# Local attention's forward scores: two heads at a time into two buffers, or four heads into one buffer of four banks

## The chip, the cores and the metric

The kernel runs on one core of one Trainium2 chip. The metric is the device time of one execution in microseconds (us); the kernel before has a median of 2354.34 us over three runs (2354.0 to 2360.47). Smaller is better. A profile is one execution taken by the hardware profiler; its times are given from the start of its span.

The engines are called by the profile's names: PE (matrix multiplication; PEld is its loading of weights, which overlaps), DVE (vector), ACT (scalar; it computes the exponentials), POOL (GpSimd) and SP, which here only issues DMAs. PSUM is the memory that PE writes its results to; it has 8 banks of 512 fp32 columns in each of 128 partitions.

## The reference

Four layers, A, B, A, B, each with a layer norm and a residual, on x of 2048 tokens by 640 features, 32 heads of 20, and then the gradients of all of it for a given gradient of the output. A is linear attention, B is causal softmax attention over a window of 256 tokens. The forward pass of B is the part that the change touches:

```python
scores = jnp.einsum("bhqd,bhkd->bhqk", q, k) * (Dh ** -0.5)
idx = jnp.arange(S)
mask = (idx[:, None] - idx[None, :] >= 0) & (idx[:, None] - idx[None, :] < W)   # W = 256
scores = jnp.where(mask[None, None], scores, -1e9)
p = _softmax(scores, axis=-1)
o = jnp.einsum("bhqk,bhkd->bhqd", p, v)
return (lambda x, *d: x.transpose(*d))(o, 0, 2, 1, 3).reshape(B, S, D) @ wo

x = A_x
x = x + _A_ref(_layernorm(x, axis=-1), A_wqkv, A_wo)
x = x + _B_ref(_layernorm(x, axis=-1), B_wqkv, B_wo)
x = x + _A_ref(_layernorm(x, axis=-1), A_wqkv, A_wo)
x = x + _B_ref(_layernorm(x, axis=-1), B_wqkv, B_wo)

_out, _vjp = jax.vjp(_f, A_x, A_wqkv, A_wo, B_wqkv, B_wo)
_grads = _vjp(grad_out)
```

## The kernel before, in words

The tokens are cut into 16 tiles of 128 rows (`TT`), and the forward pass walks over the tiles in three stretches. The first normalises each tile for layer 0 and makes its q, k and v (`a_first`, `a_qkv`). Then `ab_pass(0, False)` finishes layer 0 and does layer 1 tile by tile, and meanwhile starts layer 2 with `a_first(items, l + 2, ...)`. Last, `ab_pass(2, True)` finishes layer 2 and does layer 3; it starts no following layer, but the flips of the weights (`wflips`) that the backward pass needs belong to it. The two calls of `ab_pass` are called pass 0 and pass 2 here, by the layer they begin with.

For one tile, a pass has these pieces, each with its line: the linear attention's result (`a_num`, matmuls of L528 and of L389, `mm_ps<-mbd,pqT`), its output projection (`out_proj` with `Wo_A`, residual add L555), the layer norm (`ln`, L417 to L427), the six 320-column chunks of q, k and v of the local attention (`b_qkv`, matmuls L389 with `Wqkv_B`, evacuated by ACT L580 and DVE L578), the attention itself (`attn`), and its output projection with `Wo_B`. In pass 0 six chunks with `Wqkv_A` of the next layer stand beside them (ACT L453 and L444, DVE L454, L457 and L447). Operands are turned by DMA transposes on SP's queue (`flip`, L361).

`attn` works on a tile of 128 queries and at most three tiles of keys (`nkt` is 1 for the first tile, 2 for the second, then 3). A head has 20 features, padded to 32 rows, so that four heads, a group `g`, lie in the 128 partitions of one slice, head `hh` in the rows from 32 `hh`. There are 8 groups, `G`. A group was handled as two pairs, `p_` = 0 and 1, in these steps:

- `scores(g, p_)`: six matmuls (L605), each 128 keys by 128 queries over 32 rows, at `tile_position=(32 hh, 0)`, the two heads in two PSUM banks of an `s_ps` buffer, of which there are two; ACT's exponential of the 768 columns (L612) into an `e_sb` buffer, of which there are five; the triangular mask on the last key tile by a select on POOL (L615); the mask on the first key tile by a select on POOL for the second pair (L619), and by a multiplication with `maskT_first` on DVE for the first pair (L623).
- `values(g, p_)`: six matmuls (L646; two heads by three key tiles) of the exponentials with v, to which a column of ones is added, into one PSUM bank `pv_ps` for 16 heads. After 16 heads DVE takes the reciprocal of the sums (L653) and multiplies (L654) into `oB`, so each of these stands twice in a tile.

PSUM's eight banks are: three `mm_ps`, two `s_ps` of two banks each, one `pv_ps`. In the first stretch (layer 0) some chunks and transposes also use the `s_ps` buffers (`turn` with "s", `a_qkv`'s chunks 0 and 2).

The order is planned when the program is built. Each piece is recorded with `op(engine, duration, function, reads, writes)`; pieces get a time in units of tiles (`spread`, `items`), are sorted by it, and `Sched.order` then lays the operations out on the engines by estimated durations, an operation of PE not more than 12 places ahead of the order of priority (`AHEAD`). A `Ring` is a set of buffers used in turn; the first operation of a use waits for all operations of the use `n` places earlier. What comes out is a fixed order for each engine, and each engine carries its instructions out in that order. The planned times do not exist at run time; only the order and the semaphores do. In it, `attn`'s scores of tile `tt` are spread over the time from `tt` to `tt + 1`, and its values are the same but later by a lag of 2.1 (pass 0) or 3.1 (pass 2) of 16 steps:

```python
for part in (0, 1):
    lag = 0.001 + part * (3.1 if last else 2.1) / (2 * G)
    spread(items, tt + lag, tt + lag + 1.0, [att(i, part) for i in range(2 * G)])
```

The backward passes (from L800 on; `B_attn_bwd` has its own scores at L1324 and exponentials at L1344) are not touched.

## Time and profile before

| | |
|---|---|
| runs | 2354.34, 2354.0, 2360.47 us |
| the profiled execution | 2355.23 us, its span 2353.3 us, mean granted PE clock 0.961 |
| forward pass | 0 to about 785 us |
| pass 0, pass 2 | 148 to 484 us, 484 to 780 us |
| score matmuls L605 | 2880, 170.1 us busy |
| exponentials L612 | 512, 381.3 us busy; 813 ns with 768 columns (448 of them), 598 with 512, 385 with 256 |
| POOL's selects L615, L619 | 512 of 441 ns, 224 of 407 ns |
| DVE's mask multiplication L623 | 224 of 294 ns |
| values matmuls L646 | 2880, 148.4 us busy |

How to read it: busy times overlap across engines, and a matmul's record runs from its start to the end of its pipeline, so matmuls that follow one another overlap in the records as well. A row of the stretch windows gives the stretch, its length, each engine's busy time with its number of instructions, the granted PE clock (1.00 is full speed), the mean busy share of the DMA engines and what they moved in GB/s. A row of the timeline gives start and length in us, the engine, the line, and how many instructions of that kind follow one another; in square brackets is the idle time before it and what ended it.

### The profile page before, as it was taken

What the parts mean: (1) busy time and instruction counts of PE and PEld (TensorE: products, weight loads), DVE (VectorE), ACT (ScalarE), POOL (GpSimd) and SP (SyncE); (2) the same over time, 40 slices, a digit from 0 to 9 for tenths busy, and PEclk for the clock granted to TensorE, in tenths of its full rate; (3) what the DMA queues carried; (4) which work ended last, traced back from release to release, by engine and by line L of the source; (5) the groups of instructions that cost most, each with busy time, mean ns of one, the idle gap of its engine ahead of it and who ended that gap; (6) DMA issues with size and microseconds to landing.
All of it is one profiled execution on the core that took longest, in us unless ns stands there. A gap on an engine that the chain in (4) does not pass through costs nothing. (4 is left out here: it accounts for less than half of the span.)

```text
span 2353.3 us, 69243 instructions
## 1 busy us (share of the span) xinstructions
PE 2116.3 (90%) x28146; PEld 1438.8 (61%) x28146; DVE 1462.1 (62%) x3121; ACT 1239.7 (53%) x2093; POOL 854.1 (36%) x1852
## 2 busy tenths in 40 slices
PE   6989999879999888989889989997989888997889
PEld 4656666555555557777756557744777775664664
DVE  6756666555555579998833329803898994443552
ACT  4537777627788258888722213313888882210330
POOL 1015444405556345555512203302555551220110
PEclk9989999989999799999999989997999999998999
DMA  7759999526686867767687779637776677988973
GB/s 259 222 126 208 203 214 212 135 90 150 142 163 153 230 146 123 134 126 135 137 186 171 174 160 212 149 90 155 134 126 130 127 144 153 190 177 189 195 149 101
DMA packets 937072, 377.93 MB, mean 161 GB/s; under 512 B 817072, under 2 KB 921136, under 8 KB 936496
## 3 DMA queue, kind: packets, MB, share of 16 engines
q1 hardware_dynamic: 856672, 299.45, 63.1%
q10 hardware_dynamic: 80080, 74.06, 9.9%
q8 instruction: 220, 3.60, 0.7%
q14 instruction: 100, 0.82, 0.1%
HBM read 115.34 MB, written 114.95 MB: 98 GB/s over the span
## 5 line engine op out<-in xcount | busy, mean ns | idle before, releaser
L1344 ACT ACTIVATE e_sb<-pair 128x768 bf16<-128x768 f32 x480 | 389.0, 812 | 123.9 <-PE pair L1324 116.4
L1359 DVE TENSOR_TENSOR ds_sb<-pair,e_sb 128x768 bf16<-128x768 f32 x480 | 436.3, 948 | 18.2 <-PE pair L1324 13.7
L612 ACT ACTIVATE e_sb<-s_ps 128x768 bf16<-128x768 f32 (+2 forms) x512 | 381.3, 772 | 98.1 <-PE s_ps L605 43.0
L615 POOL TENSOR_SCALAR_AFFINE_SELECT e_sb<-e_sb 128x256 bf16<-128x256 bf16 x512 | 225.7, 441 | 466.8 <-ACT e_sb L612 461.6
L841 PE MATMUL mm_ps<-wq,dqT 128*128 128x320 bf16 x1920 | 286.9, 305 | 21.6 <-DMA dqT<-dqkv 20.2
L841 PEld LDWEIGHTS <-om 128*128 128x128 bf16 x1920 | 190.6, 100 | 170.1 <-DMA om<-o 12.9
L1351 POOL TENSOR_SCALAR_AFFINE_SELECT e_sb<-e_sb 128x256 bf16<-128x256 bf16 x448 | 182.1, 406 | 270.0 <-ACT e_sb L1344 261.3
L841 PE MATMUL mm_ps<-dqkv,om 128*128 128x480 bf16 x1280 | 271.4, 370 | 0.0
L1007 POOL TENSOR_TENSOR gw<-w,gcar 128x640 f32<-128x640 f32 x64 | 89.4, 1398 | 480.3 <-ACT w L1004 474.8
L841 PEld LDWEIGHTS <-dqT 128*128 128x128 bf16 x1920 | 187.4, 100 | 99.9 <-DMA dqT<-dqkv 24.2
L1348 POOL TENSOR_SCALAR_AFFINE_SELECT e_sb<-e_sb 128x256 bf16<-128x256 bf16 x512 | 206.4, 406 | 78.7 <-ACT e_sb L1344 77.3
L989 ACT ACTIVATE dh<-mm_ps 128x320 f32<-128x320 f32 x128 | 55.9, 437 | 334.3 <-PE mm_ps L841 290.6
L1388 PE MATMUL dqvk_ps<-Ksl,dsT 128*128 128x32 bf16 x2880 | 223.2, 177 | 3.0 <-DVE dqkv L1397 3.0
L1392 PE MATMUL dqvk_ps<-Qsl,ds_sb 128*128 128x32 bf16 x2880 | 220.2, 176 | 0.0
L1392 PE MATMUL dqvk_ps<-dOsl,e_sb 128*128 128x32 bf16 x2880 | 220.1, 176 | 0.0
L1372 PE MATMUL dsT_ps<-ident,ds_sb 128*128 128x128 bf16 x2244 | 192.2, 223 | 28.9 <-ACT dsT L1376 25.0
L1324 PE MATMUL pair<-KTg,QTg 32*128 32x384 bf16 (+2 forms) x1024 | 163.7, 324 | 41.9 <-DVE ds_sb L1359 33.0
L1376 ACT COPY dsT<-dsT_ps 128x768 bf16<-128x768 bf16 x240 | 190.9, 795 | 11.8 <-PE dsT_ps L1372 5.8
L1372 PEld LDWEIGHTS <-ds_sb 128*128 128x128 bf16 x2244 | 139.8, 99 | 92.0 <-issue 88.5
L389 PE MATMUL mm_ps<-Wqkv_B,hnTB 128*128 128x320 bf16 x960 | 179.2, 307 | 2.2 <-DMA hnTB<-hnB 1.9
L605 PE MATMUL s_ps<-QT,KT 32*128 32x128 bf16 x2880 | 170.1, 220 | 7.6 <-ACT e_sb L612 6.8
L1324 PE MATMUL pair<-VTg,dOTg 32*128 32x384 bf16 (+2 forms) x1024 | 163.8, 326 | 13.4 <-DMA dOTg<-dOpt 6.8
(155 smaller groups left out, 3734.7 us busy)
## 6 DMA issues: line engine op xcount, KB each, us to landing
qkvp<-qk_slab SPq DMA_DIRECT2D x32, 512.0 KB, 3.4
o<-o SPq DMA_DIRECT2D x64, 160.0 KB, 3.2
om<-o SPq DMA_DIRECT2D x20, 512.0 KB, 4.8
hn<-hn SPq DMA_DIRECT2D x64, 160.0 KB, 2.8
om<-hn SPq DMA_DIRECT2D x20, 512.0 KB, 5.1
qkvp<-v_slab SPq DMA_DIRECT2D x32, 256.0 KB, 2.7
dOpt<-slab ACTq DMA_DIRECT2D x32, 256.0 KB, 3.3
Ksl<-qkvp SPq DMA_DIRECT2D x16, 512.0 KB, 5.0
```

What stands on the lines that cost most here:

```text
L612: op("ACT", av(2 * nkt * P), lambda: nc.scalar.activation(e.t[:, :, 0:nkt, :], s.t[:, :, 0:nkt * P].rearrange("p h (i q) -> p h i q", q=P) ...
L615: op("POOL", 410, lambda: nc.gpsimd.affine_select(out=e.t[:, :, nkt - 1, :], in_=e.t[:, :, nkt - 1, :], compare_op=ALU.is_ge, fill=0.0, ba ...
L841: nc.tensor.matmul(ps.t[:, w0:w0 + width], lhsT=lhsT(), rhs=rhs(), start=start, stop=stop)
L1324: nc.tensor.matmul(ps[:, i, c0:c0 + len(ks) * P], lhsT=ld[g][lhs][r, q * P:(q + 1) * P], rhs=ld[g][rhs][r, ks[0] * P:(ks[-1] + 1) * P], st ...
L1344: nc.scalar.activation(e, PR[h][:, :, 0:3 * P].rearrange("p i (j q) -> p i j q", q=P), ACT.Exp, scale=self.c_att)
L1348: nc.gpsimd.affine_select(out=e[:, :, j, :], in_=e[:, :, j, :], compare_op=ALU.is_ge, fill=0.0, base=0, pattern=[[0, 2], [-1, P]], channel ...
L1351: nc.gpsimd.affine_select(out=e[:, :, j, :], in_=e[:, :, j, :], compare_op=ALU.is_ge, fill=0.0, base=-1, pattern=[[0, 2], [1, P]], channel ...
L1359: nc.vector.tensor_mul(DS[n][:, hs], PR.pop(h)[:, :, 0:3 * P].rearrange("p i (j q) -> p i j q", q=P), E[n][:, hs])
L1372: nc.tensor.transpose(ps[:, i, j, :], DS[n][:, 2 * p + i, j, :], self.ident)
L1376: (nc.vector.tensor_copy if h % 2 else nc.scalar.copy)(TSB[h], TPS.pop(h))
L1388: nc.tensor.matmul(a[:, 0, hh, :], lhsT=TSB[2 * n + hh // 2][:, hh % 2, j, :], rhs=ld[g]["K"][:, k, cs], start=(i == 0), stop=(i == len(dq ...
L1392: nc.tensor.matmul(a[:, 1 + x, hh, :], lhsT=src[n][:, hh, j, :], rhs=ld[g][rhs][:, q, cs], start=(i == 0), stop=(i == len(dkv) - 1))
```

## The change

Pairs are gone. `scores(g)` issues twelve matmuls, for each of the three key tiles the four heads in turn, into one PSUM tile `s_ps` of four banks; one exponential reads 1536 columns of it; then come the two triangular selects, each for two heads, the multiplication on DVE for the first two heads and the select of the first key tile for the other two. `values(g, p_)` stays, a pair at a time, and its reads name the half of the exponentials that it needs. The PSUM tile is a single buffer: its ring has one place. `e_sb` becomes three buffers of four heads. In the first stretch the same four banks serve as two halves (`halves`), and `follows` makes the first use of the whole tile wait for the last uses of the halves. The lag of the values becomes 3.1 steps in both passes, with 8 score pieces and 16 values pieces to a tile. An unused mask, `maskT_last`, goes, and `ones_bf` shrinks to the columns that are read.

```diff
@@ -43,8 +43,9 @@
 class Ring:
...
-    def __init__(self, n, make=None, tiles=None, name=""):
+    def __init__(self, n, make=None, tiles=None, name="", follows=None):
         self.n, self.make, self.tiles, self.items, self.name = n, make, tiles, [], name
+        self.follows = follows
...
                 if not b.ops and b.idx >= b.pool.n:
                     o.deps.update(b.pool.items[b.idx - b.pool.n].ops)
+                elif not b.ops and b.pool.follows is not None:
+                    for c in b.pool.follows.items[-b.pool.follows.n:]:
+                        o.deps.update(c.ops)
                 b.ops.append(o)
...
             PS = dict(space=bass.MemoryType.PSUM)
-            mmp, sp_ = pool("mm_ps", 3, **PS), pool("s_ps", 2, **PS)
+            mmp = pool("mm_ps", 3, **PS)
+            s_ps = pool("s_ps", **PS).tile([P, 4, 512], F32, name="s_ps")
+            halves = Ring(2, tiles=[s_ps[:, 2 * i:2 * i + 2, :].rearrange("p a b -> p (a b)") for i in range(2)])
             R = dict(
-                s=Ring(2, make=lambda: sp_.tile([P, 2, 512], F32, name="s_ps"), name="s_ps"), pv=ring("pv_ps", 1, [P, 16, 32], F32, **PS),
+                half=halves, s=Ring(1, tiles=[s_ps], follows=halves), pv=ring("pv_ps", 1, [P, 16, 32], F32, **PS),
                 mm=Ring(3, make=lambda: mmp.tile([P, 512], F32, name="mm_ps"), name="mm_ps"),
-                e=ring("e_sb", 5, [P, 2, 3, P]), QT=ring("QT", 2, [P, G, P]), KT=ring("KT", 5, [P, G, P]),
+                e=ring("e_sb", 3, [P, 4, 3, P]), QT=ring("QT", 2, [P, G, P]), KT=ring("KT", 5, [P, G, P]),
...
                     def f():
                         c0 = ci * CW
-                        ps = R["s" if l == 0 and ci in (0, 2) else "mm"].buf()
-                        if l == 0 and ci in (0, 2):
-                            ps.make = lambda: sp_.tile([P, 1024], F32, name="s_ps")
+                        ps = R["half" if l == 0 and ci in (0, 2) else "mm"].buf()
...
                 o = R["oB"].buf()
                 pvs, lv, es = {}, R["li"].buf(), {}
 
-                def products(g, p_, s):
-                    def mm_s():
-                        for j in range(nkt):
-                            for i, hh in enumerate((2 * p_, 2 * p_ + 1)):
-                                r = slice(HPAD * hh, HPAD * (hh + 1))
-                                nc.tensor.matmul(s.t[:, i, j * P:(j + 1) * P], lhsT=kTs[j].t[r, g, :],
-                                                 rhs=qT.t[r, g, :], start=True, stop=True,
-                                                 tile_position=(HPAD * hh, 0))
-                    op("PE", 200 + 50 * nkt, mm_s, [qT] + kTs, [s])
-
-                def weights(g, p_, s):
-                    e = es[g, p_] = R["e"].buf()
-                    op("ACT", av(2 * nkt * P), lambda: nc.scalar.activation(
-                        e.t[:, :, 0:nkt, :], s.t[:, :, 0:nkt * P].rearrange("p h (i q) -> p h i q", q=P),
-                        ACT.Exp, scale=self.c_att), [s], [(e, j) for j in range(nkt)])
-                    op("POOL", 410, lambda: nc.gpsimd.affine_select(
-                        out=e.t[:, :, nkt - 1, :], in_=e.t[:, :, nkt - 1, :], compare_op=ALU.is_ge, fill=0.0, base=0,
-                        pattern=[[0, 2], [1, P]], channel_multiplier=-1), [], [(e, nkt - 1)])
-                    if nkt == 3 and p_ == 1:
-                        op("POOL", 410, lambda: nc.gpsimd.affine_select(
-                            out=e.t[:, :, 0, :], in_=e.t[:, :, 0, :], compare_op=ALU.is_ge, fill=0.0, base=-1,
-                            pattern=[[0, 2], [-1, P]], channel_multiplier=1), [], [(e, 0)])
-                    elif nkt == 3:
-                        op("DVE", v2(2 * P), lambda: nc.vector.tensor_mul(
-                            e.t[:, :, 0, :], e.t[:, :, 0, :],
-                            self.maskT_first.unsqueeze(1).to_broadcast([P, 2, P])), ["masks"], [(e, 0)])
-
-                def scores(g, p_):
+                def scores(g):
                     def f():
                         s = R["s"].buf()
-                        products(g, p_, s)
-                        weights(g, p_, s)
+
+                        def mm_s():
+                            for j in range(nkt):
+                                for hh in range(4):
+                                    r = slice(HPAD * hh, HPAD * (hh + 1))
+                                    nc.tensor.matmul(s.t[:, hh, j * P:(j + 1) * P], lhsT=kTs[j].t[r, g, :],
+                                                     rhs=qT.t[r, g, :], start=True, stop=True,
+                                                     tile_position=(HPAD * hh, 0))
+                        op("PE", 210 + 55 * nkt, mm_s, [qT] + kTs, [s])
+                        e = es[g] = R["e"].buf()
+                        op("ACT", av(4 * nkt * P), lambda: nc.scalar.activation(
+                            e.t[:, :, 0:nkt, :], s.t[:, :, 0:nkt * P].rearrange("p h (i q) -> p h i q", q=P),
+                            ACT.Exp, scale=self.c_att), [s], [(e, p_, j) for p_ in (0, 1) for j in range(nkt)])
+                        for p_ in (0, 1):
+                            op("POOL", 440, lambda p_=p_: nc.gpsimd.affine_select(
+                                out=e.t[:, 2 * p_:2 * p_ + 2, nkt - 1, :], in_=e.t[:, 2 * p_:2 * p_ + 2, nkt - 1, :],
+                                compare_op=ALU.is_ge, fill=0.0, base=0, pattern=[[0, 2], [1, P]],
+                                channel_multiplier=-1), [], [(e, p_, nkt - 1)])
+                        if nkt == 3:
+                            op("DVE", v2(2 * P), lambda: nc.vector.tensor_mul(
+                                e.t[:, 0:2, 0, :], e.t[:, 0:2, 0, :],
+                                self.maskT_first.unsqueeze(1).to_broadcast([P, 2, P])), ["masks"], [(e, 0, 0)])
+                            op("POOL", 410, lambda: nc.gpsimd.affine_select(
+                                out=e.t[:, 2:4, 0, :], in_=e.t[:, 2:4, 0, :], compare_op=ALU.is_ge, fill=0.0, base=-1,
+                                pattern=[[0, 2], [-1, P]], channel_multiplier=1), [], [(e, 1, 0)])
                     return f
 
                 def values(g, p_):
                     def f():
-                        e = es.pop((g, p_))
+                        e = es[g]
                         q = 4 * g // 16
                         if q not in pvs:
                             pvs[q] = R["pv"].buf()
                         pv = pvs[q]
 
                         def mm_pv():
-                            for i, hh in enumerate((2 * p_, 2 * p_ + 1)):
+                            for hh in (2 * p_, 2 * p_ + 1):
                                 h = 4 * g + hh
                                 for j in range(nkt):
-                                    nc.tensor.matmul(pv.t[:, h % 16, :], lhsT=e.t[:, i, j, :],
+                                    nc.tensor.matmul(pv.t[:, h % 16, :], lhsT=e.t[:, hh, j, :],
                                                      rhs=vts[j].t[:, h, :], start=(j == 0), stop=(j == nkt - 1))
                         op("PE", pe([DH + 1] * 2 * nkt), mm_pv,
-                           [(e, j) for j in range(nkt)] + [(v, c) for v in vts for c in (4, 5)], [pv])
+                           [(e, p_, j) for j in range(nkt)] + [(v, c) for v in vts for c in (4, 5)], [pv])
                         if g % 4 == 3 and p_ == 1:
                             h0 = 16 * q
                             li = lambda: lv.t[:, h0:h0 + 16]
...
                             dma("ACT", lambda: self.tm_view(self.sv[l]["linv"])[:, b, :], lambda: lv.t, 16 * KB,
                                 [(lv, i) for i in range(H // 16)], [])
                     return f
-                gp = [(g, p_) for g in range(G) for p_ in (0, 1)]
-                return [scores(*a) for a in gp], [values(*a) for a in gp]
+                return [scores(g) for g in range(G)], [values(g, p_) for g in range(G) for p_ in (0, 1)]
 
             def spread(items, t0, t1, fs):
...
                         items.append((tt - 21 / 12 + i / 6, len(items), out(i)))
                         items.append((tt + 23 / 12 + i / 6, len(items), outb(i)))
                     spread(items, tt - 1.0, tt, [qkv(i) for i in range(6)])
-                    for part in (0, 1):
-                        lag = 0.001 + part * (3.1 if last else 2.1) / (2 * G)
-                        spread(items, tt + lag, tt + lag + 1.0, [att(i, part) for i in range(2 * G)])
+                    for part, lag in ((0, 0.001), (1, 3.1 / (2 * G))):
+                        spread(items, tt + lag, tt + lag + 1.0, [att(i, part) for i in range((1 + part) * G)])
                 if last:
                     spread(items, 2.0, 13.0, [wflips(t, i) for t in "BA" for i in range(4 * DT)])
                 else:
```

## The prediction

> **What bounds the kernel now.** I read the page first for where TensorE is full, then the stretch windows, then the timeline inside one tile. The change touches only the forward pass, which ends near 785 us (the last score product of `s_ps` starts at 777.5 us), the first third of these slices:
>
> ```profile
> span 2353.3 us, 69243 instructions
> ...
> PE   6989999879999888989889989997989888997889
> ...
> ACT  4537777627788258888722213313888882210330
> ...
> DMA  7759999526686867767687779637776677988973
> ```
>
> Local attention runs twice: in pass 0 (148 to 484 us, shared with the next layer's projections) and in pass 2 (484 to 780 us). Stretches in steady state, PE, PEld, DVE, ACT and POOL in this order, then clock and DMA:
>
> ```profile
> 300.00:420.00 120.00, 118.63 (x1665) 73.72 (x1663) 81.99 (x234) 94.92 (x166) 59.37 (x142) 1.00 0.97 211
> 660.00:740.00 80.00, 79.91 (x1259) 47.52 (x1257) 46.31 (x135) 66.83 (x105) 48.91 (x120) 1.00 0.75 159
> ```
>
> PE is busy 98.9% and 99.9% at full clock, ACT 79% and 84%. In pass 0 the DMA share is 0.97 too. So TensorE's instruction stream sets the pace. To get the time of a 128-row tile I count the reciprocals of L653, two per tile, with both ends inside each window:
>
> ```profile
> 197.40:404.60 207.20, 5.14 (x21) 1.00 0.97 209
> 404.60:460.40 55.80, 1.64 (x7) 0.97 0.63 151
> 551.80:750.60 198.80, 5.92 (x25) 1.00 0.71 151
> 671.10:735.30 64.20, 2.01 (x9) 1.00 0.74 158
> 750.60:780.00 29.40, 1.02 (x5) 0.76 0.64 198
> ```
>
> 21 reciprocals are ten tiles: 20.7 us each in pass 0, and three more in its tail at 18.6. In pass 2 twelve tiles take 16.6 each, the last four of the steady ones 16.05, and the two at the end 14.7. Inside a tile:
>
> ```profile
> 303.61 0.84 PE L389 MATMUL mm_ps<-Wqkv_B,hnTB 128*128 128x320 bf16 x5
> 304.38 0.34 PE L605 MATMUL s_ps<-QT,KT 32*128 32x128 bf16 x6
> 304.65 0.31 PE L646 MATMUL pv_ps<-v_slab,e_sb 128*128 128x32 bf16 x6
> 304.82 0.84 PE L389 MATMUL mm_ps<-Wo_A,oTA 128*128 128x320 bf16 x5
> 305.59 0.34 PE L605 MATMUL s_ps<-QT,KT 32*128 32x128 bf16 x6
> 305.86 0.32 PE L646 MATMUL pv_ps<-v_slab,e_sb 128*128 128x32 bf16 x6
> ...
> 306.03 0.81 ACT L612 ACTIVATE e_sb<-s_ps 128x768 bf16<-128x768 f32 x1 [0.16 <-PE s_ps L605]
> ```
>
> Rows overlap because a matmul's record includes its latency, so I price by starts. Five 320-column matmuls: one lasts 0.30, so starts are (0.84-0.30)/4 = 0.135 apart. From the start of five to the start of the values matmuls is 1.04 us, twice; less 5 x 0.135 leaves **0.365 us for one score batch**. Only 0.125 of it is streaming (0.34 less the 0.214 that one score matmul lasts; three pairs, about 0.06 a pair). The other 0.24 is spent entering and leaving the 32-row form; the trace shows the same hole as weight loads that stand 0.26 us for no semaphore ("issue", 109.5 us over 393 batches of L605).
>
> **The change, part by part.**
>
> *Score batches.* 16 batches of six matmuls per tile become 8 batches of twelve. Removed: eight entries and exits. The trace has no four row groups at once. Lower bound of the cost: four stream as two do (the members of a pair stand within a few ns of each other), a batch stays 0.365, and a group saves 0.365, a tile 8 x 0.365 = 2.9 us. Upper bound: twelve matmuls stream as six pairs, a batch is 0.365 + 3 x 0.063 = 0.555, and a tile saves 8 x (0.73-0.555) = 1.4 us. I take the lower cost: the pair already shows that matmuls of different row groups do not wait for one another. The Trainium skill, "TensorE: Matmul & The Clock Gate", section Part 3: Packing small matmuls, says that matmuls in distinct 32-row groups run concurrently, about 4 ns apart, and gives 3.07x for four; by it the saving is 2.9 us, by pairs 1.4.
>
> *The exponential.* L612 takes 813 ns for 768 columns and 598 for 512, so 0.84 ns a column; 1536 columns take 813 + 768 x 0.84 = 1.455 us. Two of 768 take 1.51 back to back (570.78 us), so ACT gains next to nothing (0.06 us a group). ACT is not the bound, so I count it at nothing.
>
> *One buffer instead of two.* This is the added wait: scores of group g+1 can start only when the exponential of g has ended. Queued behind the waiting matmul on PE are the values of g, the projections, and with them DVE's and ACT's evacuations. The loop, from rows: exponential 1.455; to the first score matmul about 0.06 (an exponential of 570.78 + 0.81 = 571.59, then this row), batch 0.34, to the next exponential 0.10 (305.59 + 0.34 = 305.93, then 306.03).
>
> ```profile
> 570.78 1.51 ACT L612 ACTIVATE e_sb<-s_ps 128x768 bf16<-128x768 f32 x2 [1.00 <-PE s_ps L605]
> ...
> 571.65 0.34 PE L605 MATMUL s_ps<-QT,KT 32*128 32x128 bf16 x6 [0.20 <-ACT e_sb L612]
> ```
>
> That is 1.95 us a group, 15.6 a tile (2.14 and 17.1 if as pairs). ACT's other work fits in the 0.5 us between exponentials: evacuations of 0.43 us overlap their neighbours by 0.1 at each end.
>
> *Pass 0.* PE alone: 20.7-2.9 = 17.8 us a tile, above the loop's 15.6, and the PE work between two batches in the built order is even (1.64 to 1.94 us a group), so the loop is covered. If the cover failed, each group would pay the excess over 17.8/8 = 2.2 us. What comes near next is DMA. 209 GB/s x 20.7 us = 4.33 MB a tile; the built order carries about half a weight flip less per tile (0.16 MB), so 4.17 MB in 17.8 us is 234 GB/s, against 211 in the longest full stretch and 222 in the fullest 20 us. At 211 a tile takes 19.8 us, at 222 18.8. Bounds 17.8 to 19.8; I take 18.5, because the present stretch has no PE wait for a DMA, so some slack is there. Saving 2.2 x 10 = **22 us**. The tail's three tiles have less to interleave: 18.6 becomes about 17.3, **4 us**.
>
> *Pass 2.* PE alone: 16.05-2.9 = 13.1, so the loop takes over at 15.6. In the built order three of eight groups carry 1.66 us of other matmuls plus 0.365: 2.03, each 0.08 over the loop; a tile is 15.8 at best. Bounds: 15.8 (0.8 under today's 16.6) to 17.1 (as pairs, 0.5 over). I take 16.3: **12 x 0.3 = 4 us** saved. The two last tiles have no projections left to fill with: 14.7 becomes the loop's 15.8, **2 us lost**.
>
> *Moved without cost.* Masks on POOL: the same 24 a tile, 10 us of 18, now in threes of 1.27 us behind each exponential; the values of the second pair wait for the third one and stand after at least one chunk of projections (0.68), which covers most of it. The mask multiply stays one a group on DVE (82 of 120 us busy). Three buffers of four heads hold more than five of two. The later slot of pass 0's values and the layer-0 use of the same banks as two halves add no instruction; SP's and ACT's DMAs are the same in number. The dropped mask saves one 128x128 memset and one POOL select, once.
>
> Sum: -22 -4 -4 +2 = **-28**. The profiled execution took 2355.2 us (span 2353.3 and 1.9 around it), 0.9 over the runs' median of 2354.3: 2327.
>
> **The rivals.**
>
> *Full gain* (12%): DMA gives way and both passes reach their floors. Pass 0 -29, tail -6, pass 2 12 x -0.8 = -10, end +2: 2311. For it: no DMA wait on PE now; against: 0.97.
>
> *DMA takes the place of PE in pass 0* (13%): tile 19.8, so -9, tail -2, pass 2 -2: 2341. For it the share of 0.97 in exactly that stretch, against it that in pass 2 the share is 0.71.
>
> *Four do not run at once* (11%), so the change doesn't do what it says: pass 0 at 19.4, -13, tail -2, pass 2 at the pairs' loop 17.1, +6, end +5: 2350. For it: no row with four groups.
>
> *The single buffer makes it slower* (14%). PE executes in order: if the values of g, waiting for POOL's selects, and a chunk of 0.68 stand ahead of the next scores, the scores come late by d, and nothing else can feed ACT. The third select ends 0.44 + 0.41 + 0.41 = 1.27 us after the exponential (L615, L619); plus values 0.17 and a chunk it is 2.1, so d of 0.2 is near at hand in some groups. A tile is then t = 15.6 + 8d wherever that is the longest. Pass 2 loses from d = 0.12. Over 10 + 3 + 12 + 2 tiles the sum 27t stands against 207.2 + 55.8 + 198.8 + 29.4 = 491, so the whole loses from t = 18.2, d = 0.33. At d = 0.4, t = 18.8: +16, 2370. Against it: the built order spreads this work evenly in pass 0. The Trainium skill, "Perfetto Trace Analysis", section Optimizing Tensor Performance, speaks for it: groups should rotate through different banks so that one's evacuation overlaps the next one's matmuls. Today's trace agrees (PE waits only 6.8 us in 13 places for L612); the change gives just that up.
>
> **How the numbers follow.** Forecast 2327 at 50%, its own range 2315 to 2340. About 0.3% (7 us) can be told from no change. Faster: the forecast, the full gain and most of the DMA case, 0.70. Same: the pairs case and what is left of DMA's, 0.16. Slower: 0.14. Eight in ten: 2306, just under the full gain, to 2360, over the pairs case and short of most of the slower one.
>
> **What would show it.** A score batch of twelve lasts 0.34 to 0.36 us from first start to last end (right), 0.5 or more (pairs). L612 is 256 instructions, 1.455 us at full size. A tile of pass 0 takes 17.8 to 19, with PE still over 95% busy; if PE falls to 90% and waits for flips (`hnTB`, `QT`, `KT`), DMA took over. In pass 2 PE is some 85% busy and its idle time stands before L612's scores, released by ACT; with a tile over 17 us the slower rival is true. What lies behind 790 us should only move, not change. The forecast is wrong at the root if batches cost less than 0.24 us to enter and leave once alone, or if PE's clock, which fell to half at the end of pass 2 (0.76 in the last window above), falls in the steady part with the thinner PE work.

## The result, and the profile after

The changed kernel takes 2366.6 us (median of 7 runs, 2361.5 to 2370.7), the kernel before on the same chip 2354.6 (7 runs): ratio 1.0052, 95% interval 1.0032 to 1.0071. It is slower by half a per cent, where 2327 us was forecast. The profiled execution took 2366.6 us, its span is 2364.9, the mean granted clock 0.957.

From its page, the total and the same three rows of slices:

```profile
span 2364.9 us, 68753 instructions
...
PE   5778888878888789898889979997989888997899
...
ACT  3527777716777328888822213312888882210330
...
DMA  7659999726666766777687779736666677878963
```

TensorE lost its nines in the first third: it is no longer full there, and yet nothing is faster. The stretch windows (PE, PEld, DVE, ACT, POOL, clock, DMA share, GB/s), and two windows of the reciprocals L653:

```profile
300.00:420.00 120.00, 106.49 (x1677) 70.12 (x1675) 82.98 (x238) 88.23 (x120) 59.03 (x144) 0.99 0.95 205
660.00:740.00 80.00, 67.91 (x1180) 46.14 (x1178) 47.67 (x128) 61.96 (x62) 46.91 (x114) 0.96 0.70 141
...
209.60:417.00 207.40, 4.75 (x21) 0.98 0.97 203
574.80:767.00 192.20, 5.83 (x23) 0.95 0.68 144
```

In pass 0 PE falls from 98.9% to 88.7% busy, and 21 reciprocals still take 207 us, ten tiles of 20.7: the work that was saved became waiting. In pass 2, 23 reciprocals are eleven tiles of 17.4 us, where the kernel before took 16.5. That the batches do cost less can be read from the timeline of PE:

```profile
303.72 0.84 PE L394 MATMUL mm_ps<-Wqkv_B,hnTB 128*128 128x320 bf16 x5
304.49 0.35 PE L612 MATMUL s_ps<-QT,KT 32*128 32x128 bf16 x12
304.77 0.43 PE L532 MATMUL mm_ps<-mbd,pqT 128*128 128x320 bf16 x3
```

From 303.72 to 304.77 are 1.05 us; less five chunks' starts of 0.135 a batch of twelve costs 0.375 us. A batch of six cost 0.365.

Cut at the ends of every second reciprocal, the spans divide so (us):

| | to the end of tile 0 | pass 0, 15 tiles | to tile 0 of pass 2 | pass 2, 15 tiles | rest |
|---|---|---|---|---|---|
| before | 166.6 | 293.8 | 77.3 | 242.5 | 1573.0 |
| after | 178.3 | 293.6 | 69.6 | 259.6 | 1563.7 |
| difference | +11.7 | -0.2 | -7.7 | +17.1 | -9.3 |

So there are three questions: why the first stretch grew by 11.7 us although no score is computed there, why pass 0 gained nothing inside, and why pass 2 lost 17.

**First stretch.** PE's rows stand in the same order as before, but it waits at new places. Timeline of PE after:

```profile
30.20 0.57 PE L394 MATMUL s_ps<-Wqkv_A,hnTA 128*128 128x320 bf16 x3 [0.58 <-DVE pp L461]
31.55 0.43 PE L394 MATMUL s_ps<-Wqkv_A,hnTA 128*128 128x320 bf16 x2 [0.78 <-ACT hnTA L416]
```

The second row is the rest of the same five-matmul sum as the first. In the middle of an accumulation it waits for ACT's copy of `hnTA`, which reads the other half of the four banks. The first theory (shared tile): the framework takes the two halves, views of one tile, for one buffer.

**Pass 0.** ACT's timeline with the DMA issues of its queue (ACTq), and one row of SP's queue:

```profile
302.74 1.45 ACT L617 ACTIVATE e_sb<-s_ps 128x1536 bf16<-128x1536 f32 x1
303.75 0.33 ACTq L362 DMA_DIRECT2D r<-rt  x1
306.01 0.34 ACTq L362 DMA_DIRECT2D v<-vv  x1
306.40 0.42 ACT L584 CAST v_slab<-mm_ps 128x320 bf16<-128x320 f32 x1 [2.21 <-PE mm_ps L394]
306.57 0.34 ACTq L362 DMA_DIRECT2D o<-oA  x1
306.72 1.46 ACT L617 ACTIVATE e_sb<-s_ps 128x1536 bf16<-128x1536 f32 x1
...
301.23 1.15 SPq L362 DMA_DIRECT2D WqTA<-wT  x1
```

The scores of 304.49 are done at 304.84, and the exponential starts at 306.72. The bracket blames PE, but what stands in front is the store of `v`, issued at 306.01. The trace has for each DMA the semaphore that tells of its landing. That of `v` is the one that the store `WqTA<-wT` uses too, which landed at 305.92, and `v` is issued 0.1 us after. In the traces all DMAs of the two queues use eight such semaphores in turn, so a store on ACT waits for the landing of the DMA eight places earlier, on whichever queue. Before, `v` followed another store of ACT on its semaphore; after, the new order puts a weight flip or its store there, and `ek` behind the flip `hnTA`. From 195 to 415 us 17 stores of ACT are issued within 0.35 us after such a landing, and ACT had stood idle 22.5 us before them; before there were 6, with 4.0 us. Over 10.6 tiles that is 2.1 us a tile, just what 18.5 lacks to 20.7.

**Pass 2.** ACT again:

```profile
608.26 1.45 ACT L617 ACTIVATE e_sb<-s_ps 128x1536 bf16<-128x1536 f32 x1 [0.60 <-POOL e_sb L621]
609.72 0.33 ACTq L362 DMA_DIRECT2D linv<-li  x1
610.09 0.42 ACT L584 CAST qk_slab<-mm_ps 128x320 bf16<-128x320 f32 x1 [0.38 <-DVE li L653]
610.25 1.23 ACTq L362 DMA_DIRECT2D o<-oB  x1
611.60 1.45 ACT L617 ACTIVATE e_sb<-s_ps 128x1536 bf16<-128x1536 f32 x1 [1.08 <-DVE x L559]
```

The next scores are done at 610.11. But the store of `o` takes 1.23 us to issue, and the next exponential, queued behind it, starts 1.89 us after the last one's end. The second theory (held queue): with one buffer nothing but the next exponential lets PE go on, and ACT's queue carries stores that hold it. The rival for pass 0 is the prediction's own: transfers, at a share of 0.95 to 0.97, bind.

### The profile page after: what moved, and what is told of

Same layout as the page of the kernel before. It is cut to its first block, busy times and chain, and to the rows that moved or that the text cites. A ratio compares the mean times of both kernels' runs of the same rounds, so it can differ in the third digit from the quotient of the medians.

```text
span 2364.9 us, 68753 instructions
## 1 busy us (share of the span) xinstructions
PE 2054.9 (87%) x28146; PEld 1428.7 (60%) x28146; DVE 1472.1 (62%) x3120; ACT 1219.0 (52%) x1837; POOL 850.2 (36%) x1851
## 5 line engine op out<-in xcount | busy, mean ns | idle before, releaser
L617 ACT ACTIVATE e_sb<-s_ps 128x1536 bf16<-128x1536 f32 (+2 forms) x256 | 350.8, 1370 | 86.2 <-PE s_ps L612 42.9
L621 POOL TENSOR_SCALAR_AFFINE_SELECT e_sb<-e_sb 128x256 bf16<-128x256 bf16 x512 | 217.9, 448 | 491.1 <-ACT e_sb L617 467.0
L839 PE MATMUL mm_ps<-wq,dqT 128*128 128x320 bf16 x1920 | 284.9, 304 | 20.7 <-DMA dqT<-dqkv 20.7
L839 PEld LDWEIGHTS <-om 128*128 128x128 bf16 x1920 | 190.3, 100 | 166.5 <-DMA om<-o 9.9
L1349 POOL TENSOR_SCALAR_AFFINE_SELECT e_sb<-e_sb 128x256 bf16<-128x256 bf16 x448 | 182.1, 406 | 272.2 <-ACT e_sb L1342 263.6
L1346 POOL TENSOR_SCALAR_AFFINE_SELECT e_sb<-e_sb 128x256 bf16<-128x256 bf16 x512 | 206.5, 406 | 76.6 <-ACT e_sb L1342 75.2
L394 PE MATMUL mm_ps<-Wqkv_B,hnTB 128*128 128x320 bf16 x960 | 185.7, 312 | 3.8 <-ACT v_slab L584 2.9
L646 PEld LDWEIGHTS <-e_sb 128*128 128x128 bf16 x2880 | 131.1, 98 | 80.7 <-POOL e_sb L629 19.0
```

What stands on the lines that cost most here:

```text
L394: nc.tensor.matmul(ps.t[:, w0:w0 + width], lhsT=lhsT(), rhs=rhs(), start=start, stop=stop)
L617: op("ACT", av(4 * nkt * P), lambda: nc.scalar.activation(e.t[:, :, 0:nkt, :], s.t[:, :, 0:nkt * P].rearrange("p h (i q) -> p h i q", q=P) ...
L621: op("POOL", 440, lambda p_=p_: nc.gpsimd.affine_select(out=e.t[:, 2 * p_:2 * p_ + 2, nkt - 1, :], in_=e.t[:, 2 * p_:2 * p_ + 2, nkt - 1, ...
L839: nc.tensor.matmul(ps.t[:, w0:w0 + width], lhsT=lhsT(), rhs=rhs(), start=start, stop=stop)
L1346: nc.gpsimd.affine_select(out=e[:, :, j, :], in_=e[:, :, j, :], compare_op=ALU.is_ge, fill=0.0, base=0, pattern=[[0, 2], [-1, P]], channel ...
```

## The experiments

The ratios compare with runs of the kernel before on the same chip. The other columns are us of the profiled execution, in the stretches of the table above. "Held" is ACT's idle time directly before stores that were issued within 0.35 us after the landing of the earlier DMA on their semaphore, from 195 to 400 us (after 20.2, before 4.0).

| | first | pass 0 | held | between | pass 2 | rest | ratio (95%) |
|---|---|---|---|---|---|---|---|
| e1 | 163.8 | 293.7 | 21.2 | 68.0 | 259.7 | 1573.2 | 1.0007 (0.9992 to 1.0022) |
| e2, five | 179.8 | 289.5 | 16.4 | 70.5 | 260.5 | 1564.0 | 1.0023 (1.0011 to 1.0035) |
| e2, all | 179.8 | 309.8 | 0 | 70.3 | 246.2 | 1575.5 | 1.0108 (1.0088 to 1.0128) |
| e4 | 165.8 | 292.2 | 22.4 | 70.1 | 246.0 | 1573.4 | 0.9954 (0.9936 to 0.9972) |
| e5 | 165.0 | 276.1 | 3.2 | 69.3 | 255.6 | 1588.1 | 1.0002 (0.9987 to 1.0018) |
| e6 | 162.9 | 290.5 | 16.1 | 70.4 | 243.9 | 1571.1 | 0.9929 (0.9906 to 0.9952) |
| e7 | 166.3 | 284.8 | 16.7 | 70.9 | 246.3 | 1566.0 | 0.9886 (0.9867 to 0.9905) |
| e8 | 168.9 | 281.4 | 16.0 | 71.7 | 236.1 | 1567.9 | 0.9856 (0.9834 to 0.9878) |
| e9 | 166.7 | 309.0 | 12.8 | 70.4 | 265.4 | 1562.0 | 1.0073 (1.0047 to 1.0100) |
| e10 | 192.2 | 270.4 | 1.5 | 71.0 | 235.1 | 1566.9 | 0.9928 (0.9908 to 0.9947) |
| e11 | 193.5 | 280.3 | 2.9 | 69.4 | 246.2 | 1563.4 | 0.9998 (0.9984 to 1.0013) |
| e12 | 166.5 | 272.9 | 1.4 | 70.6 | 235.7 | 1568.8 | 0.9817 (0.9795 to 0.9839) |
| e13 | 165.7 | 280.6 | 4.4 | 71.3 | 236.1 | 1564.9 | 0.9839 (0.9818 to 0.9861) |
| b1 | 167.1 | 294.4 | 4.2 | 77.0 | 234.6 | 1579.6 | 0.9999 (0.9984 to 1.0014) |
| b2 | 168.9 | 294.0 | 4.6 | 76.9 | 235.7 | 1570.3 | 0.9947 (0.9928 to 0.9966) |
| b3 | 190.6 | 291.1 | 0 | 77.2 | 234.6 | 1570.0 | 1.0043 (1.0028 to 1.0059) |

**e1: the halves as tiles of their own.**

```diff
-            s_ps = pool("s_ps", **PS).tile([P, 4, 512], F32, name="s_ps")
-            halves = Ring(2, tiles=[s_ps[:, 2 * i:2 * i + 2, :].rearrange("p a b -> p (a b)") for i in range(2)])
+            halves, whole = Ring(2, make=lambda: hp.tile([P, 1024], F32, name="s_ps")), []
+
+            def banks():
+                if not whole:
+                    hst.close()
+                    whole.append(pool("s_ps", **PS).tile([P, 4, 512], F32, name="s_ps"))
+                return whole[0]
...
-                half=halves, s=Ring(1, tiles=[s_ps], follows=halves), pv=ring("pv_ps", 1, [P, 16, 32], F32, **PS),
+                half=halves, s=Ring(1, make=banks, follows=halves), pv=ring("pv_ps", 1, [P, 16, 32], F32, **PS),
...
+            hst = ExitStack()
+            hp = hst.enter_context(tc.tile_pool(name="fw_half", bufs=2, **PS))
```

> The changed kernel, but the first stretch's two halves are two PSUM tiles of their own, given back before the four-bank tile is made. Theory of the shared tile (TensorE waits in the first stretch for readers of the other half, because both halves are one tile): the first score product starts at about 148 us, as in the kernel before, not at 160.3; the rest only moves; total 2366.6 - 11.7 = 2355 us, no loss left against the kernel before. Rival (the first stretch is longer for another reason, such as the masks on POOL or the clock): first score product stays near 160 us and the total at 2366 us.

The first score starts at 145.4 us and the ratio falls from 1.0052 to 1.0007, 10.6 us. The shared tile is the first stretch's whole loss. The waits of PE's chunks there for the readers of a half shrink from 19.1 to 4.5 us, and the stretch from 178.3 to 163.8; from the waits of PE up to 145 us (us in total, times, longest), after and then e1 (its L401 is L394):

```profile
PE s_ps L394 <- DVE pp L461: 6.5, 11, 1.8
PE s_ps L394 <- ACT pqT L416: 5.5, 6, 1.0
PE s_ps L394 <- ACT hnTA L416: 4.5, 6, 0.8
...
PE s_ps L394 <- DVE pk L461: 2.6, 7, 0.7
```

```profile
PE s_ps L401 <- ACT hnTA L423: 3.1, 3, 2.1
...
PE s_ps L401 <- DVE pk L468: 1.4, 5, 0.4
```

**e2: stores off ACT's queue.** First the five of `a_qkv` in pass 0, then all nine of a tile in both passes.

```diff
-                                dma("ACT", lambda: self.tm_view(sv["v"])[:, tt, :], lambda: vv[:, tt, :], 160 * KB,
+                                dma("SP" if l else "ACT", lambda: self.tm_view(sv["v"])[:, tt, :], lambda: vv[:, tt, :], 160 * KB,
                                     [("vv", tt, 4), ("vv", tt, 5)], [])
...
```

> The changed kernel, but in pass 0 the stores of v, pk, ek, pq and eq are issued from SP's queue, not ACT's. Theory of the held queue (ACT's exponentials stand behind stores that wait for a flip to land, because both use one of eight DMA semaphores; 22.5 us of ACT's idle time from 195 to 415 us end just after such a store, and with one buffer nothing else feeds the loop): a group in pass 0 falls from 2.55 us to about 2.3, a tile from 20.6 to about 18.5, total about 2345 us. Rival theory (DMA at a share of 0.97 binds pass 0): a tile stays at 20.6, TensorE or ACT waits for flips instead, total 2363 to 2370 us.

> The changed kernel, but all nine stores that ACT issues in a tile of the passes are issued from SP's queue. Held queue: pass 0 as with five moved or a little better, and pass 2, where ACT's idle time before exponentials ends after the store of o in 11 groups of 103 (9 us), gains some 5 to 10 us as well; total about 2337 us. Rival (DMA binds, or SP's queue is now the one that is held): flips leave later, PE waits for QT, KT or hnTB, total 2366 us or more.

With five moved a tile takes 20.06 us (tiles 2 to 12), a small gain between the two theories: the remaining stores are held for 16.4 us instead. With all nine moved the total goes the rival's way. Pass 2 runs at 16.3 us a tile, 13 us less, but pass 0 gets slower by 16: now SP's queue is held, the flips behind it leave late, and PE waits 16.3 us for `hnTB` from 195 to 415 us. The queue that issues a store pays for what it waits for.

**e4: e1, and only pass 2's four stores on SP.**

> The changed kernel with the two halves as tiles of their own and, in pass 2 alone, the four stores of a tile (r32, o of layer 2, o and linv of layer 3) on SP's queue. Theory (pass 2 lost because ACT carries each store's issue of some 0.34 us in line with the exponentials, and with one buffer nothing covers it): pass 2's steady tile falls from 17.4 to 16.3 us as it did with all stores moved, its 15 steps from 259.6 to about 246, pass 0 stays at 20.6 a tile, total 2366.6 - 10.6 - 13 = 2343 us, so faster than the kernel before. Rival (pass 2 gained there only because pass 0 ended otherwise, and the loop itself takes 17.4): 2356 us.

As the held queue says: 2344 us by the ratio, pass 2 at 246.0. After and e4 in the same window of pass 2:

```profile
560.00:700.00 140.00, 119.15 (x1999) 79.35 (x1998) 79.71 (x215) 103.32 (x103) 77.77 (x189) 0.93 0.65 142
```

```profile
560.00:700.00 140.00, 119.68 (x2180) 81.84 (x2178) 86.92 (x236) 110.94 (x113) 84.04 (x205) 1.00 0.72 154
```

181 more matmuls and 7.6 us more of ACT's work in the same 140 us, and the clock is back at 1.00. A group takes 2.05 us: exponential 1.45, to the first score 0.14, batch 0.35, to the next exponential 0.11 (means of its rows).

**b1 and b2: the same stores moved in the kernel before**, in b2 without those of the last two tiles.

```diff
-                            dma("ACT", lambda: self.tm_view(self.sv[l]["o"])[:, b, :], lambda: o.t, 160 * KB, ks, [])
+                            dma("SP" if l == 3 and b < TT - 2 else "ACT", lambda: self.tm_view(self.sv[l]["o"])[:, b, :], lambda: o.t, 160 * KB, ks, [])
...
```

> The kernel before (pairs, two buffers) with the same four stores of pass 2 moved to SP's queue. Theory (the issue of stores on ACT only costs where one buffer leaves the exponentials uncovered): TensorE bounds pass 2 there at 99% busy, so nothing changes, ratio 0.998 to 1.002. Rival (a store on ACT costs in any form of the loop): pass 2 gains 10 us or more, ratio 0.996 or less, and e4's gain says nothing on four heads at once.

> The kernel before with pass 2's stores on SP, except those of the last two tiles. In b1 pass 2 took 234.6 instead of 242.5 us, and 8 us were lost again between the last tile and the first backward exponential (77.0 instead of 69.0 us). If that loss is the store of the last linv in SP's queue: 69 us again, total 8 us under the kernel before, ratio 0.9965. If the backward pass starts at a time that something else sets (the weights' loads, the gradient's): no gain, ratio 1.000.

Here the theory was wrong in part. The pairs gain too, 8 us in pass 2 (16.5 to 16.0 us a tile), so a store on ACT costs also where two buffers stand ready, about 0.6 of what it costs with one (7.9 against 13.7). b1 shows it in no total, because the last `linv` then holds SP's queue for 13.8 us (16.4 in e4) and the backward pass starts 8 us later; b2 mends it, and the kernel before becomes 0.5% faster without four heads at once.

**e5, e6 and e7: pass 0.** e5 is e4 with the weight flips, which the built order draws into pass 0, held back until pass 2. e6 is e4 with e2's five stores. e7 is e4 with `pk` and `eq` of pass 0 moved as well, and the last two tiles' stores of pass 2 left on ACT as in b2.

```diff
-                    flip(lambda: b.t, lambda: wsb[key][:, et, c0:c0 + D], 160 * KB, keys, [b])
+                    flip(lambda: b.t, lambda: wsb[key][:, et, c0:c0 + D], 160 * KB, keys + [("mbd", 0)], [b])
```

> As e4, and the flips of the weights (which the built order draws forward into pass 0) wait until pass 2. If transfers bound pass 0 (a DMA share of 0.95 to 1.00): the lighter pass 0 gains 4 to 8%, a tile from 20.6 to 19 to 19.8 us, total 10 to 20 us under e4. If ACT's held queue alone bounds it, it gains only by what the weight flips held (v's store, some 1.5 us a tile in 9 tiles), with the DMA share falling to 0.9 and a tile at about 19.5 as well, but then ACT's idle time before stores shows it. If neither, a tile stays at 20.6 and pass 2 pays for the flips.

> As e4, and in pass 0 the five stores of the next layer's projections go to SP's queue too. With five moved alone a tile of pass 0 took 20.06 instead of 20.6 us at a DMA share of 1.00 and the total fell by about 7 us; the sum of the parts is 2366.6 - 10.6 - 13 - 6 = 2337 us. If SP's queue becomes the limit: above 2345 us.

> As e4 (halves apart, pass 2's stores on SP), and in pass 0 only the stores of pk and eq are on SP's queue: in the order as built this leaves seven stores a tile on ACT, but none behind a late flip on its semaphore, and the transfers stay the same. The last two tiles' stores of pass 2 are back on ACT (on SP, the last linv held SP's queue for 16 us and TensorE waited 7.4 us for om at the start of the backward pass). Held semaphore theory for pass 0: ACT's 23 us before stores from 195 to 415 us fall under 6, a tile from 20.5 to 18.7 us, total about 2349.3 - 27 - 8 = 2315 us. DMA theory: a tile stays at 20 us or more with a DMA share of 0.98 to 1.00, and only the 8 us at the start of the backward pass are gained: about 2337 us.

e5 gains 16 us in pass 0 (19.0 us a tile) with held time and DMA share both down, and loses 24 again: 9.6 in pass 2 and 14.7 at the start of the backward pass, whose loads come late. e6 came out at 2338 us by its ratio, as added up. e7 fits neither theory: the total fell to 2328 us, but the tile stayed at 20.05. `v` now stood behind `pk` on its semaphore, and `pk`, in SP's queue, landed late: 16.7 us held. e7 is the best form with one buffer in both passes.

**e8: four heads at once in pass 0, pairs in pass 2. e9: e7 with two exponentials of 768.**

```diff
+            R["s2"] = Ring(2, make=pair, follows=R["s"])
...
-                return [scores(g) for g in range(G)], [values(g, p_) for g in range(G) for p_ in (0, 1)]
+                if l == 3:
+                    return ([scores2(g, p_) for g in range(G) for p_ in (0, 1)],
+                            [values(g, p_) for g in range(G) for p_ in (0, 1)])
+                return [scores(g) for g in range(G)], [values(g, p_) for g in range(G) for p_ in (0, 1)]
...
```

```diff
-                        op("ACT", av(4 * nkt * P), lambda: nc.scalar.activation(
-                            e.t[:, :, 0:nkt, :], s.t[:, :, 0:nkt * P].rearrange("p h (i q) -> p h i q", q=P),
-                            ACT.Exp, scale=self.c_att), [s], [(e, p_, j) for p_ in (0, 1) for j in range(nkt)])
+                        for p_ in (0, 1):
+                            op("ACT", av(2 * nkt * P), lambda p_=p_: nc.scalar.activation(
+                                e.t[:, 2 * p_:2 * p_ + 2, 0:nkt, :], s.t[:, 2 * p_:2 * p_ + 2, 0:nkt * P].rearrange(
+                                    "p h (i q) -> p h i q", q=P),
+                                ACT.Exp, scale=self.c_att), [s], [(e, p_, j) for j in range(nkt)])
```

> As e7, but pass 2 scores pairs into two buffers of two banks again (four heads at once in pass 0 only). If the single buffer's loop of 2.05 us a group is what bounds pass 2 in e4 (16.35 us a tile), pairs with their TensorE bound of 16.0 us a tile are faster: 15 steps from 246 to 235 us, total 9 to 11 us under e7. If pass 2 is bound by something both share (stores, selects on POOL, transfers), it stays at 246 us and the total is the same as e7's within 3 us.

> As e7, but the four heads' exponential is two of 768 columns. By the rows before, two take 1.51 and one 1.455 us, so where the loop bounds (pass 2) a group takes 2.10 instead of 2.05 us, a tile 16.8 instead of 16.35, total +7 us and more. Rival: the first pair's selects start 0.7 us earlier and the values of a group wait less for POOL, so pass 2 stays at 246 us or gains. (Pass 0 is not compared: there the built order changes which stores share a semaphore.)

`scores2` scores a pair, as the kernel before did. e8: pass 2 falls by 10 us to 236.1. Cleared of the stores, pairs take 16.0 us a tile and the single buffer 16.3, so four at once is the worse form there. e9: pass 2 rises by 19 us, a tile from 16.3 to 17.7, more than the 0.45 that eight times 0.06 gives. The built order changed too (it puts values that wait for the masks ahead of the scores), so the 1.3 us are not all the exponential's; but one exponential of 1536 is no loss.

**e10, e11, b3: no weight flips in pass 0, because they are issued in the first stretch**, in three forms: e8 (e10); one buffer in both passes with all nine stores of pass 0 on ACT and pass 2's on SP as in e7 (e11); and b2 (b3).

```diff
-                    b = R["wT"].buf()
+                    b = R["hnTB"].buf()
...
+            spread(items, 3.6, 15.0, [wflips(t, i) for t in "AB" for i in range(4 * DT)])
             run(items)
             a_kv(0)
...
```

> As e8 (four at once in pass 0, pairs in pass 2), and the flips of the weights are issued in the first stretch, in buffers of hnTB that stand unused there, so that none is left for pass 0. DMA theory (211 GB/s is what pass 0's transfers reach, and 4.2 MB a tile then take 20 us): without the weight flips a tile falls from 19.8 to about 19.0 us, as with the flips held back to pass 2, and nothing is paid for them elsewhere: total 2354.6 x 0.9856 - 10 = about 2311 us. If the single buffer's loop with ACT's stores holds pass 0: it stays at 19.8 us with the DMA share down to 0.9, total 2320 us.

> The changed kernel with halves apart, pass 2's stores on SP (the last two tiles' on ACT), the flips of the weights in the first stretch, and all nine stores of pass 0 on ACT as in the changed kernel. DMA theory: a tile of pass 0 falls from 20.5 to about 19.0 us although every store is still issued by ACT, total about 2316 us. Theory that the stores' issue on ACT is what holds pass 0: a tile stays above 20 us, total about 2335 us.

> The kernel before as b2 (pass 2's stores on SP but for the last two tiles), with the flips of the weights in the first stretch. TensorE was 99% busy in pass 0 with pairs, so there the transfers were not the limit: a tile stays at 20.7 us and the total at b2's 2342 us (ratio 0.994 to 0.996). If transfers already held the pairs: a tile under 20.2 us, ratio 0.991 or less. e11 against this run is then what four heads at once bring when both kernels are cleared of what stood in their way.

All three totals came out 23 to 38 us above what was expected, in the main for one reason: the first stretch grows by 22 to 28 us. There PE waits longer for `hnA` (23.7 us in e11 up to 150 us, 15.8 in e8) and for ACT's copy into `vv` (8.2 us); what holds these stays open. In pass 0 itself a tile takes 18.7 us in e10 and 19.4 in e11, where 19.0 was expected of both. With pairs (b3) it takes 20.4, between the two theories (20.7 and under 20.2) and 0.5 less than in b2.

**e12: e8 with the A weights' flips between the passes. e13: e12 with 512 KB more a tile.**

```diff
             ab_pass(0, False)
+            for i in range(4 * DT):
+                wflips("A", i, "hnTB")()
...
```

```diff
+                        if ci == 3 and l == 1:
+                            dma("SP", lambda: self.tm_view(self.spare)[:, tt, :], lambda: qk.t, 512 * KB,
+                                [(qk, i) for i in range(4)], [])
```

> As e8 (four at once in pass 0, pairs in pass 2), and the 20 flips of the A weights, which were drawn into pass 0, are recorded between pass 0 and pass 2 in buffers of hnTB; the 20 of the B weights stay in the first stretch's gaps. DMA theory: pass 0's steady tile falls from 19.8 to about 18.5 us as in e10 (DMA share under 0.9), while the first score product stays at 148 to 151 us, where e10 paid 24 us for its hn stores behind the flips; between the passes up to 5 us more. Total 2354.6 x 0.9856 - 13 + 3 = about 2311 us, ratio 0.980 to 0.984. If it pays between the passes what it gains in pass 0: ratio 0.986, as e8.

> As e12, with one more store of 512 KB a tile in pass 0 (qk_slab written a second time, to a place that nothing reads), which puts back more bytes than the weight flips of pass 0 were (some 0.5 MB a tile) but no flip that a store of ACT shares its semaphore with. Theory of bytes (211 GB/s bind at 4.2 MB): a tile goes back from 18.4 to 20 us, total up by 20 us to about 2337 us. Theory of held stores (e8's 16 us of ACT's idle time before stores against e12's 1.4 us): a tile stays at 18.4 to 18.9 us, ACT's held time under 4 us, total up by less than 6 us.

e12 pays nothing elsewhere and is the fastest form found, 0.9817. e13 tests the rival. From 220 to 400 us: e8, e12, e13 and b3 in turn:

```profile
220.00:400.00 180.00, 163.98 (x2581) 107.93 (x2580) 128.72 (x367) 134.78 (x182) 88.68 (x220) 0.99 1.02 212
```

```profile
220.00:400.00 180.00, 172.44 (x2761) 114.52 (x2759) 136.64 (x386) 143.82 (x196) 95.54 (x235) 1.00 0.95 201
```

```profile
220.00:400.00 180.00, 170.57 (x2728) 113.20 (x2728) 135.65 (x384) 141.63 (x193) 93.67 (x231) 1.00 1.01 228
```

```profile
220.00:400.00 180.00, 177.96 (x2512) 111.15 (x2514) 125.26 (x356) 142.92 (x249) 89.08 (x212) 1.00 0.79 179
```

e13 moves 228 GB/s, 8% more than e8, and runs a tile in 18.85 us (tiles 2 to 12; half of them in 18.3 to 18.6) against e8's 19.83. So 211 GB/s did not bind. What fell with the weight flips is the held time, from 16.0 us to 1.4 and 4.4 (under 4 was expected of e13): over some ten tiles 1.4 and 1.1 us a tile, and a tile is 1.1 and 1.0 us shorter. In e8 the stores wait, nearly all, for the landing of `pk` (before `v`) and of the flip `KT` (before `o`), not of a weight flip; without the weight flips the semaphores are dealt out anew, and `o` stands behind ACT's own `ek`. b3 shows the other side: with pairs PE is 98.9% busy with a DMA share of 0.79, so there neither held.

Two limits of e13. Its extra store is not free: pass 0 as a whole takes 7.7 us more than in e12 and only 0.8 less than in e8, most of it in the first two steps and the last. And it puts back the bytes, not all of the DMA engines' time: share times tile is 20.2 us in e8, 17.8 in e12 and 19.0 in e13, for the weight flips go in smaller packets (the mean packet is 444 bytes in e8, 500 in e12, 550 in e13). That the engines' time, not the bytes, held e8 is thus not excluded by e13. Against it stands that the list of PE's waits in e8 from 220 to 400 us names no DMA, and that the flips of the activations land no later there (`KT` 3.8 us from issue to landing, in e12 3.7, in e13 3.8; `hnTB` 3.5, 3.8, 3.6).

## Why the prediction failed, point by point

- *Score batches*: right. 0.375 us for twelve matmuls against 0.365 for six, and PE's busy time fell from 118.6 to 106.5 in the 120 us window.
- *The exponential*: 1.45 us as worked out, and it belongs in the loop where it was put.
- *Moved without cost, "the layer-0 use of the same banks as two halves add no instruction"*: failed, 11 us. True of instructions, but halves that are views of one tile got waits that two tiles do not have (e1). This term, put at nothing, is all that the kernel became slower by: without it the ratio is 1.0007.
- *Moved without cost, "SP's and ACT's DMAs are the same in number"*, and in the loop *"ACT's other work fits in the 0.5 us between exponentials"*: failed, and this is where the forecast gain went. The number is the same, but these stores stand in ACT's queue, and they wait: for DVE's results and long issues in pass 2 (13.7 us, e1 to e4), and in pass 0 for DMAs with which the new order makes them share a semaphore (about 2 us a tile). The forecast counted ACT's evacuations and left out its DMA issues.
- *Pass 0, DMA as what comes near next*: as the limit that was priced, 211 to 222 GB/s, wrong, and the rival "DMA takes the place of PE" with it. PE fell to 88.7% busy, as that rival's sign said, but what it waited for was ACT's exponential (25.1 us from 148 to 480 us), not the flips. That its 19.8 us a tile was near e7's 20.05 is luck. e13 moved more bytes in less time (that the DMA engines' time played no part is argued, not shown). The tile of 18.5 itself can be reached: e12 shows 18.7, most tiles 18.3 to 18.4, though with some 0.4 MB a tile less to move than was forecast; e13, with 4.3 MB, 18.85.
- *Pass 2*: 16.3 was forecast, and e4, e6 and e7 show 16.3 to 16.4. The number is partly luck: the loop was priced at 1.95 us a group with an allowance above it, and it takes 2.05 in every group, because the first score starts 0.14 us after the exponential, not 0.06. And the 16.6 it was set against was not PE's floor: without the stores the pairs take 16.0. At the end of the pass, where 2 us were to be lost, the last two tiles take 33.4 us in e4 against 29.4 before.
- *The single buffer makes it slower* came true in its sign (a tile of pass 2 over 17 us), not in its mechanism, and its 2370 us, near the 2366.6 measured, is luck. PE late by POOL's selects and a chunk is a small part: in e4, selects and all, a score starts 0.14 us after its exponential. What was late was ACT.
- *PE's clock*, named as what would make it wrong at the root, did fall in pass 2, but with the waits: in e4 it stays at full speed from 560 to 748 us. How much of the 13.7 us the slower clock cost, and how much the waits themselves, was not separated.
- *Pass 0's tail*, three tiles, was to gain 4 us; it gained 0.8 (55.8 to 55.0). Between the passes 7.7 us were gained that the forecast does not have; every form with four heads at once in pass 0 has them (68.0 to 71.7 us, with pairs 76.9 to 77.3).
- The rest of the span, whose code is the same, ended 9.3 us shorter. Over the other runs it lies between 1562 and 1588 us, so that is no gain of the change. In e5 and b1 late loads and a held queue lengthen it; why it moves otherwise stays open.

The sum of what went otherwise: first stretch +11.7, pass 0 with its tail -0.2 instead of -26, between the passes -7.7, pass 2 +17.1 instead of -2, rest -9.3: 40 us, 2366.6 less 2327.

## What to carry to other kernels

A buffer taken out of a loop makes every wait in the queue of the engine that feeds it part of the loop: list all that the engine issues, stores too, and for each what it waits for. When one tile is to serve as several buffers, make them tiles of their own, and after any reordering look at which DMAs now share a semaphore, since a store can end up waiting for a transfer that it has nothing to do with. Compare a new form with the old one only after the same obstacles are out of both: here, with the stores of both in the same places, four heads at once is worth 1.0 us a tile in pass 0 (e11 against b3, 19.4 and 20.4) and costs 0.3 in pass 2 (16.3 against 16.0), and the change as made showed neither. With `pk` and `eq` on SP too, four at once take 18.7 (e10); pairs were not run so, but with PE 98.9% busy in b3 they have by an estimate at most some 0.2 us a tile left to gain (1.1% of 20.4).

## What the runs showed of the hardware

**Clock.** After, the granted clock drops to half for 3.41 us seven times from 560 to 740 us, though PE is 85% busy there and its longest gap from 540 to 760 us is 1.57 us. In the 3.41 us before each drop PE was busy 1.8 to 2.4 us. In e4, just as busy on the whole, no gap from 560 to 735 us exceeded 0.8 us, and no drop came; cut into the same steps of 3.41 us as the clock's record, no step had PE busy for less than 2.5 us. That is no threshold: in the changed kernel itself steps with 2.2 and 2.4 us (from 628 and 717 us) were followed by no drop. The Trainium skill, "TensorE: Matmul & The Clock Gate", section A second HAM failure mode: psum-queue depth-cycling, tells of clocks that swing because of many short idle times between groups of matmuls; the trace agrees. The section HAM oscillation before it gives the rule as no idle gap above some 3.4 us; these drops came with gaps of half that.

**Issuing DMAs.** Moving four stores a tile from ACT to SP made the kernel before 0.5% faster (b2), and moving nine made the changed one slower (e2). The Trainium skill, "DMA: Bandwidth & Descriptors", section Issuing engines are not separate DMA queues, says that the choice of the issuing engine only saves the sequencer's time, which is usually small. The runs agree that the transfers did not change (before and b2 move 154 and 158 GB/s from 560 to 700 us, at a share of 0.75 both), and put a price on that time: an issue is 0.33 us, sometimes 1.2, and in the changed kernel a wait of up to 2.8 us stands before it.

**DMA share.** The mean busy share of the DMA engines does not tell how many bytes they can move: from 300 to 420 us e8 moves 212 GB/s and e13 229, both at a share of 1.03. From 220 to 400 us the mean packet is 444 bytes in e8 (38.15 MB in 85863 packets) and 550 in e13 (41.06 MB in 74682).
